# The second batch element's sums of weights begin only behind its token mixing

## The chip, the cores and the metric

One core of a Trainium2 chip. The metric is the device time of one execution, in microseconds (us); the median of the runs before is 1364.33. The core has a matrix engine (TensorE, PE), three engines for elementwise work (VectorE or DVE, ScalarE or ACT, GpSimd or POOL), a queue that only issues transfers (SyncE, SP), and sixteen DMA engines that carry the transfers out.

## What is computed

All numbers are float32. Twelve heads of attention with normalised queries and keys, for a batch of 8 elements of 448 positions, then a block that mixes over positions (tokens) and then over the 768 channels:

```python
# q, k, v: (8, 12, 448, 64)
q_n, k_n = rmsnorm(q, g_q), rmsnorm(k, g_k)
attn = softmax(q_n @ k_n.T / 8)
x = (attn @ v), heads side by side          # (8, 448, 768)
h = relu(x.T @ w_tok1) @ w_tok2             # token mixing, width 256
u = x + h.T
out = u + relu(u @ w_ch1) @ w_ch2           # channel mixing, width 1536
```

## The kernel before

The kernel works through the batch elements one after the other. While element b goes through token and channel mixing, the attention of element b + 1 is computed beside it. The order of the instructions on PE, DVE, ACT and POOL is written out by the program: work is cut into items, each a pair of a cost in us and a function that emits instructions. `merge` (L27) deals several lists of items into one so that each advances in proportion to its total cost. `run` (L120) emits a list, and emits outputs and bridge transfers that were put off with `later` when the sum of costs has passed their time. SP's instructions are put in order by the framework, by when their waits can be met. Each transfer, whether SP or ACT issues it, uses one of eight completion counters in turn, and waits until the previous transfer on that counter has landed.

From the second element on, channel mixing uses a scheme of seven half-size products in place of eight (`PRODUCTS`, L648). For it the four quarters of each weight matrix must also be combined into four sums and differences. The first element still multiplies by the plain quarters; meanwhile the weights are stored to device memory by quarters (slots 0 to 3). `sum_items` (L196) makes the combined slots (4 to 7) of 36 weight pieces, in 39 items. Item i loads piece i (L203, 256 KB, into one of five buffers of `raw_pool`), combines piece i - 2 with three POOL instructions (L206, L207, L209), and stores piece i - 3 (L211, 256 KB). Items 0 to 5 run at the end of the first element's main stage, items 6 to 11 with its last items, items 12 to 32 and then 33 to 38 beside the second element.

Weights in use are read back from device memory in units of 384 KB by `load_units` (L676, transfer L687), up to five units ahead of the one in use; a unit with combined weights isn't loaded ahead before its pieces are stored.

The stages of an element from the second on:

- token mixing: `tok1` (matmul L629, then a Relu on ACT, L632), in two halves, and six `tok2` (matmul L637, then an addition into the element's state by DVE, L642). After every second one, `moving_sums` (L650) makes combinations of the state, two on DVE and two on POOL (L660, L661). The turned output of the element before (DVE, L855) is stored by ACT in four transfers each (L577). This part is the list `begin`, but for the first half of `tok1`, which runs ahead of it.
- channel-up: 21 items `ch1` (L749, matmul L761), three groups of seven products, each with two or three combinations on DVE, POOL and ACT (L766 and others). This is the list `early`.
- channel-down: 14 items `ch2` (L803, matmul L818) for two thirds of the columns (the list `double`), and 7 for the last third.

Beside these run attention's steps: scores (L334), their exponentials on ACT (L338), values (L408), row sums of the exponentials on POOL and DVE (es, L376), and for later heads the loads of q, k and v (L1071, L287) and the inverse root mean squares: squares on ACT (L1090), a reduction (L1104), halves put together (L1112, L1121) and a Newton iteration (L1126 to L1147) on DVE. PE's results of both mixings go through two PSUM buffers (`ps_M`, L99).

Of the kernel before, what the change touches and what calls it, by code (L numbers as in the profile page):

```python
# [26 lines left out]
def merge(*lists):  # L27

    totals = [sum(c for c, _ in l) or 1.0 for l in lists]
    done = [0.0] * len(lists)  # L30
    at = [0] * len(lists)
    res = []
    while True:
        live = [i for i in range(len(lists)) if at[i] < len(lists[i])]
        if not live:
            return res
        i = min(live, key=lambda i: (done[i] + lists[i][at[i]][0] / 2) / totals[i])
        c, fn = lists[i][at[i]]
        at[i] += 1
        done[i] += c  # L40
        res.append((c, fn))
# [3 lines left out]
def whole(ctx, tc, shifted, pre, q, k, v, g_q, g_k, moe_w_tok1, moe_w_tok2, moe_w_ch1, moe_w_ch2, out):  # L45
# [74 lines left out]
    def run(items):  # L120
        for c, fn in items:
            fn()
            clock[0] += c
            while pending and pending[0][0] <= clock[0]:
                pending.pop(0)[1]()
# [70 lines left out]
    def sum_items():  # L196


        def one(i):
            n = len(stages)  # L200
            if i < n:
                t = st["sum", i] = raw_tile()
                nc.sync.dma_start(out=eight(t)[:, 0:4], in_=slots(i, 0, 4))  # L203
            if 0 <= i - 2 < n:
                q = eight(st["sum", i - 2])
                nc.gpsimd.tensor_tensor(out=q[:, 6], in0=q[:, 1], in1=q[:, 0], op=ALU.subtract)  # L206
                nc.gpsimd.tensor_tensor(  # L207
                    out=q[:, 4:6], in0=q[:, 1:7:5], in1=q[:, 3:4].to_broadcast([P, 2, P]), op=ALU.add)
                nc.gpsimd.tensor_tensor(out=q[:, 7], in0=q[:, 2], in1=q[:, 5], op=ALU.subtract)  # L209
            if 0 <= i - 3 < n:  # L210
                nc.sync.dma_start(out=slots(i - 3, 4, 8), in_=eight(st.pop(("sum", i - 3)))[:, 4:8])  # L211
                st["summed"] = i - 3 if i - 3 < n - 1 else n
                load_units(st["at"])

        def eight(t):
            return t[:].rearrange("p n w -> p (n w)").bitcast(F32).rearrange("p (q n) -> p q n", q=NQ)
        return [(1.0, lambda i=i: one(i)) for i in range(len(stages) + 3)]
# [43 lines left out]
    def weight_items(lo, hi):  # L261

        def one(i):
            if 3 <= i and i + 2 < len(chunks):
                weight_load(i + 2)
            convert_bits(i - 2)
            if i < len(chunks):
                convert_first(i)
            if 0 <= i - 1 < len(chunks):
                convert_second(i - 1)  # L270
            if 0 <= i - 2 < len(chunks):
                convert_last(i - 2)
            if 0 <= i - 3 - len(first):
                store(i - 3 - len(first))
        return [(1.0, lambda i=i: one(i)) for i in range(lo, hi)]
# [582 lines left out]
    def turns(b, cs):  # L858
        return [(0.3, lambda cc=cc: trans_y(b, cc)) for cc in cs]
# [3 lines left out]
    def x_items(b, h):  # L863
        return [(0.1, lambda j=j: trans_x(b, j)) for j in range(h * NC // 2, (h + 1) * NC // 2)]

    def tok1_items(b, h):
        return [(us(NS, HC), lambda j=j, h=h: tok1(b, j, h)) for j in range(NJ)]

    def middle_items(b):

        items = []
        for t in range(KC):
            items += [(us(NJ, S), lambda cc=cc: tok2(b, cc)) for cc in (t, KC + t)]
            if b:
                items.append((0.0, lambda t=t: moving_sums(b, t)))
        if b == 0:
            items += [(us(6, S), lambda mp=mp, o=o, j=j: ch1_first(mp, o, j))
                      for mp in range(KF // 2) for o in range(2) for j in range(2)]
            return items, [(us(6, S), lambda o=o, h=h, m=m: ch2_first(o, h, m))
                           for o in range(2) for h in range(2) for m in range(2)]  # L880
        items += [(us(6, HS), lambda mp=mp, i=i: ch1(b, mp, i)) for mp in range(KF // 2) for i in range(7)]
        return items, [(us(6, HS), lambda i=i, j=j: ch2(b, 0, i, j)) for i in range(7) for j in range(2)]

    def in_next(b):


        return b < B - 1 and not shifted

    def last_items(b, sums):

        single = [(us(6, HS), lambda i=i: ch2(b, 1, i, 0)) for i in range(7)]
        if b == 0:
            single = merge(
                [(us(6, S), lambda o=o, h=h: ch2_first(o, h, 2)) for o in range(2) for h in range(2)], sums)
        l = [] if in_next(b) else turns(b, [0, 1, KC, KC + 1])
        return [single[0]] + merge(single[1:-1], l) + [single[-1]]
# [52 lines left out]
    left, sums = [], sum_items()  # L949
    for b in range(B):  # L950
        early, double = middle_items(b)
        if b == 0:
            begin = x_items(0, 1) + tok1_items(0, 0) + tok1_items(0, 1)
            early = merge(begin + early, weight_items(BEFORE, then)) + merge(
                double, weight_items(then, len(chunks) + 3) + sums[:6])
        else:

            run(merge(tok1_items(b, 0), left[:2]))
            begin, early = merge(tok1_items(b, 1) + early[:3 * KC], left[2:]), early[3 * KC:]
            if b == 1:  # L960
                early, double = merge(begin + early, sums[12:33]), merge(double, sums[33:])
                begin = []
            early = begin + early + double
        lo = (b + AHEAD) * per + 1
        att = []
        if b + AHEAD < B:
            att = att_items(lo, lo + 10) + x_items(b + AHEAD, 0) + att_items(lo + 10, lo + per)
        tail = 4
        early, last = early[:-tail], early[-tail:]
        if b + 1 < B:  # L970
            last = merge(last, x_items(b + 1, 1))
        run(merge(att, early) + last + last_items(b, sums[6:12]))
        left = turns(b, range(NC) if in_next(b) else [2, KC + 2])
# [182 lines left out]
def kernel(  # L1156
# [30 lines left out]
    with tc.If(nc.values_load(small[0:1, 0:1], min_val=0, max_val=1,  # L1187
                              skip_runtime_bounds_check_because="a comparison's result") > 0) as arm:
        whole(tc, False, pre, *args)
    with arm.Else():  # L1190
        whole(tc, True, pre, *args)
# [30 lines left out]
```

## Time and profile before

| | us |
|---|---|
| runs: median of 4 (lowest, highest) | 1364.33 (1355.04, 1370.91) |
| the profiled execution | 1367.82 |
| its span, first to last instruction | 1366.0 |
| PE busy, share of the span | 1287.4, 94% |
| DVE, POOL, ACT busy | 749.8, 369.7, 366.2 |
| mean traffic of the DMA engines | 175 GB/s |

The costliest groups of instructions that bear on the change, with their busy time in the whole span:

| group | times | busy us, mean ns |
|---|---|---|
| PE, channel-down products (L818) | 1764 | 343.9, 355 |
| PE, channel-up products, moving side from the combinations (L761) | 1008 | 201.6, 355 |
| PE, `tok2` (L637) | 192 | 81.9, 567 |
| POOL, middle instruction of a sum (L207) | 36 | median 726 ns each |
| transfers: unit from device memory (L687) | 318 | 3.9 us from issue to landing |
| transfers: load of a piece (L203) | 36 | 4.7 us |
| transfers: store of a sum (L211) | 36 | 4.0 us |

How to read it: the times of a group are of one profiled execution. Idle time on an engine counts only where the chain of work that ends last goes through it, so a stage is judged by what PE waits for in it. The granted clock is the share of its full clock that PE had. The share of the DMA engines is the mean of the sixteen.

### The profile page before, as it was taken

What the parts mean: (1) busy time and instruction counts of PE and PEld (TensorE: products, weight loads), DVE (VectorE), ACT (ScalarE), POOL (GpSimd) and SP (SyncE); (2) the same over time, 40 slices, a digit from 0 to 9 for tenths busy, and PEclk for the clock granted to TensorE, in tenths of its full rate; (3) what the DMA queues carried; (4) which work ended last, traced back from release to release, by engine and by line L of the source; (5) the groups of instructions that cost most, each with busy time, mean ns of one, the idle gap of its engine ahead of it and who ended that gap; (6) DMA issues with size and microseconds to landing.
All of it is one profiled execution on the core that took longest, in us unless ns stands there. A gap on an engine that the chain in (4) does not pass through costs nothing.

```text
span 1366.0 us, 20203 instructions
## 1 busy us (share of the span) xinstructions
PE 1287.4 (94%) x7408; PEld 924.3 (68%) x7408; DVE 749.8 (55%) x1295; ACT 366.2 (27%) x734; POOL 369.7 (27%) x406
## 2 busy tenths in 40 slices
PE   4889999979998999999999999999999989999997
PEld 2344444437687578785888667785878758787997
DVE  6988987226773465626574275635566155443212
ACT  5553442023220243203331133302332023200100
POOL 1202110347662233203330132312341024211220
PEclk9999999999999999999999999999999999999998
DMA  9685878988899566694559755694667835375555
GB/s 202 187 242 169 243 184 214 248 209 212 240 245 229 125 163 149 152 231 89 145 132 212 173 131 140 154 225 97 161 168 162 213 71 162 111 185 149 180 165 122
DMA packets 508144, 238.83 MB, mean 175 GB/s; under 512 B 374084, under 2 KB 466628, under 8 KB 508036
## 3 DMA queue, kind: packets, MB, share of 16 engines
q1 hardware_dynamic: 416962, 225.97, 64.0%
q10 hardware_dynamic: 90946, 11.48, 5.3%
q8 instruction: 61, 1.00, 0.3%
q14 instruction: 47, 0.39, 0.1%
q0 software_dynamic: 128, 0.00, 0.0%
HBM read 197.85 MB, written 39.52 MB: 174 GB/s over the span
## 4 chain that ended last, share of the span: by engine, by line
PE 75%; DVE 8%; DMA 7%; SPq 2%; issue 2%; ACT 2%; ACTq 1%; POOL 1%; DVEq 0%; POOLq 0%
PE m_ps L761 23%; PE m_ps L818 19%; PE s_ps L334 8%; PE o_ps L408 7%; PE m_ps L629 6%; DMA unit<-ws 5%; PE m_ps L742 4%; PE m_ps L724 4%; PE m_ps L637 2%; SPq L1071 1%; PE d_ps L388 1%; ACTq L577 1%; DVE uT L642 1%; DMA ws<-raw 1%; DVE es L376 1%
## 5 line engine op out<-in xcount | busy, mean ns | idle before, releaser
L818 PE MATMUL m_ps<-hb,unit 128*128 128x224 f32 x1764 | 343.9, 355 | 18.1 <-DMA unit<-ws 17.6
L818 PEld LDWEIGHTS m_ps<-hb,unit 128*128 128x128 f32 x1764 | 330.7, 190 | 36.9 <-issue 30.1
L761 PE MATMUL m_ps<-tu,unit 128*128 128x224 f32 x1008 | 201.6, 355 | 2.7 <-DVE hb L766 2.4
L761 PEld LDWEIGHTS m_ps<-tu,unit 128*128 128x128 f32 x1008 | 188.9, 190 | 18.7 <-issue 5.6
L338 ACT ACTIVATE e<-s_ps 128x448 f32<-128x448 f32 x336 | 157.1, 547 | 133.8 <-PE s_ps L334 99.4
L761 PE MATMUL m_ps<-uT,unit 128*128 128x224 f32 x756 | 152.3, 355 | 0.3 <-DVE uT L642 0.3
L761 PEld LDWEIGHTS m_ps<-uT,unit 128*128 128x128 f32 x756 | 141.4, 190 | 14.8 <-DVE qkT L314 7.0
L334 PE MATMUL s_ps<-qkT 64*64 64x448 f32 x1260 | 148.2, 558 | 2.3 <-ACT x L609 1.7
L408 PE MATMUL o_ps<-e,v 64*64 64x448 f32 x1316 | 149.3, 540 | 0.1
L827 POOL TENSOR_TENSOR uT<-uT,r 128x448 f32<-128x448 f32 (+1 forms) x56 | 50.6, 914 | 278.0 <-DVE r L827 146.8
L827 DVE TENSOR_TENSOR uT<-uT,m_ps 128x448 f32<-128x448 f32 (+1 forms) x70 | 33.8, 500 | 144.9 <-PE m_ps L818 144.9
L766 DVE TENSOR_TENSOR r<-m_ps,r 128x448 f32<-128x448 f32 x63 | 39.2, 623 | 131.1 <-PE m_ps L761 80.8
L376 DVE TENSOR_TENSOR es<-es,e 128x896 f32<-128x896 f32 x84 | 97.3, 1159 | 10.3 <-ACT e L338 7.4
L637 PE MATMUL m_ps<-w_sb,h 128*128 128x448 f32 x192 | 81.9, 567 | 17.0 <-DVE uT L642 14.1
L408 PEld LDWEIGHTS o_ps<-e,v 64*64 64x64 f32 x1316 | 50.0, 133 | 68.2 <-issue 62.4
L376 POOL TENSOR_TENSOR es<-e 128x896 f32<-128x896 f32 x21 | 44.3, 2111 | 190.7 <-ACT e L338 190.7
L1104 DVE TENSOR_REDUCE ms<-sq 128x28 f32<-128x896 f32 (+2 forms) x47 | 51.3, 1091 | 81.0 <-ACT sq L1090 78.3
L334 PEld LDWEIGHTS s_ps<-qkT 64*64 64x64 f32 x1260 | 44.2, 135 | 74.3 <-issue 60.8
L629 PE MATMUL m_ps<-x,w_sb 112*128 112x384 f32 x256 | 86.0, 490 | 0.0
L766 POOL TENSOR_TENSOR hb<-r,r 128x448 f32<-128x448 f32 x21 | 23.8, 1135 | 225.4 <-ACT r L782 225.4
L637 PEld LDWEIGHTS m_ps<-w_sb,h 128*128 128x128 f32 x192 | 35.6, 194 | 60.1 <-DVE uT L642 28.9
L317 ACT ACTIVATE qkT<-qkT,g_t 128x448 f32<-128x448 f32 x36 | 24.0, 668 | 194.3 <-DVE qkT L314 182.9
(100 smaller groups left out, 1360.3 us busy)
## 6 DMA issues: line engine op xcount, KB each, us to landing
unit<-ws SPq DMA_DIRECT2D x318, 384.0 KB, 3.9
raw<-in_moe_w_ch_dram SPq DMA_DIRECT2D x72, 256.0 KB, 3.7
out_dram<-turned ACTq DMA_DIRECT2D x192, 56.0 KB, 1.9
v<-in_v_dram SPq DMA_DIRECT2D x94, 112.0 KB, 4.9
xs<-xt SPq DMA_DIRECT2D x56, 168.0 KB, 4.3
x<-xs SPq DMA_DIRECT2D x14, 672.0 KB, 7.3
ws<-stage SPq DMA_DIRECT2D x36, 256.0 KB, 3.9
raw<-ws SPq DMA_DIRECT2D x36, 256.0 KB, 4.7
```

The source lines that it names most:

```text
L334: nc.tensor.matmul(out=pss[i][rows_of(i, a), 0:S], lhsT=qkT[h, 1, k * D:(k + 1) * D], rhs=qkT[h, 0, :], start=True, stop=True)
L338: nc.scalar.activation(out=e[:, i, :], in_=pss[i][:, 0:S], func=AF.Exp)
L376: eng.tensor_tensor(out=es[:], in0=(es if k > 1 else st["e", t, 0])[:], in1=st["e", t, k][:], op=ALU.add)
L408: nc.tensor.matmul(out=st["o", p][a * D:(a + 1) * D, 0:S], lhsT=vt[rows, k * D:(k + 1) * D], rhs=e[rows, :], **kw)
L629: nc.tensor.matmul(out=ps[:, 0:HC], lhsT=w1_sb[0:R, c, jc * P:(jc + 1) * P], rhs=st["x", b, h][0:R, :, c, :], start=(c == 0), stop=(c == N ...
L637: nc.tensor.matmul(out=ps[:, 0:S], lhsT=st["h1", jc][:, cc * P:(cc + 1) * P], rhs=w2_sb[:, jc].rearrange("p c r -> p (c r)"), start=(jc == ...
L724: nc.tensor.matmul(out=ps[:, 0:S], lhsT=st["w"][t // KC][:, t % KC, j, :], rhs=u[:, t, :], start=(t == 0), stop=(t == 2 * KC - 1))
L742: nc.tensor.matmul(out=ps[:, 0:S], lhsT=w, rhs=natural(half)[:, :, t, :], start=(half == 0 and t == 0), stop=(half == 1 and t == KF - 1))
L761: nc.tensor.matmul(out=ps[:, j * HS:(j + 1) * HS], lhsT=w[:, t, j, :], rhs=m, start=(t == 0), stop=(t == KC - 1))
L766: add = lambda e, o, x, y: e.tensor_tensor(out=o, in0=x, in1=y, op=ALU.add)
L818: nc.tensor.matmul(out=ps[:, j * HS:(j + 1) * HS], lhsT=st["w"](j, t), rhs=hb[:, HB[what], t, :], start=(t == 0), stop=(t == KF - 1))
L827: add = lambda e, o, x, y: e.tensor_tensor(out=o, in0=x, in1=y, op=ALU.add)
```

## The change

The items 12 to 32 of the sums were dealt among the items of token mixing and channel-up together (`begin + early`); now they are dealt among those of channel-up alone, and token mixing stands ahead of them without any. Nothing is added or left out.

```diff
             run(merge(tok1_items(b, 0), left[:2]))
             begin, early = merge(tok1_items(b, 1) + early[:3 * KC], left[2:]), early[3 * KC:]
             if b == 1:
-                early, double = merge(begin + early, sums[12:33]), merge(double, sums[33:])
-                begin = []
+
+                early, double = merge(early, sums[12:33]), merge(double, sums[33:])
             early = begin + early + double
```

The joined list is then dealt together with the attention of the third element, `run(merge(att, early) + ...)` (L972), in which an item of the sums counts with a cost of 1.0.

## The prediction

> **What bounds the kernel now.** I read the page first: TensorE (PE) is busy 94% of the span, so only stages in which it is not can give or lose much. Then busy time by stage. The second batch element (b = 1) runs from 275.0 to 450.4 us; I cut it at its first token matmul (L629), first channel-up matmul (L761) and first channel-down matmul (L818), and its last stretch where no attention is left. The third element, which does the same work without sums, is cut alike. Columns: stretch, length, busy us of PE, its weight loads, VectorE (DVE), ScalarE (ACT), GpSimd (POOL), granted clock, busy share of the DMA engines, GB/s.
>
> ```profile
> 275.00:314.40 39.40, 32.30 (x146) 14.15 (x144) 17.07 (x34) 7.53 (x18) 18.51 (x24) 0.91 0.74 190
> 314.40:385.66 71.26, 67.92 (x433) 53.69 (x430) 44.60 (x67) 25.46 (x53) 47.08 (x63) 1.00 0.92 240
> 385.66:428.50 42.84, 42.31 (x264) 34.41 (x263) 30.94 (x46) 8.29 (x17) 21.96 (x25) 1.00 0.95 238
> 428.50:450.40 21.90, 16.67 (x84) 15.74 (x85) 2.71 (x7) 0.34 (x1) 2.58 (x4) 1.00 0.97 254
> ...
> 450.40:480.40 30.00, 29.05 (x145) 13.21 (x144) 16.41 (x34) 7.48 (x18) 8.45 (x6) 1.00 0.39 76
> 480.40:547.06 66.66, 66.66 (x433) 53.61 (x430) 39.92 (x68) 25.63 (x52) 22.66 (x16) 1.00 0.66 163
> ```
>
> Token mixing takes 39.4 us with sums beside it and 30.0 us without; channel-up 71.3 against 66.7. So the sums cost 9.4 us in the one and 4.6 in the other, and the DMA engines are almost full through the whole second element (0.92, 0.95, 0.97). Next the chain of waits through the hole in token mixing (start, us, what):
>
> ```profile
> 287.80 5.56 DMA unit<-ws
> 293.35 0.02 issue
> 293.37 3.71 DMA out_dram<-turned
> 297.08 0.94 ACT sq L1090
> ...
> 298.04 1.10 DVE ms L1104
> ...
> 302.54 0.54 DVE uT L642
> 303.08 0.04 issue
> 303.13 5.73 PE m_ps L637 x10
> ```
>
> PE stands still until 303.13 for the first addition of token mixing (L642). This is queued on DVE behind the reduction L1104 and a square-root chain, which wait for ACT's squares, which are queued behind ACT's issue of output stores; those wait for earlier transfers. Last, what SP, the queue of nearly all transfers, waits for in channel-up, second element, then third:
>
> ```profile
> SPq L687 <- PE m_ps L761: 5.0, 5, 1.9
> ...
> SPq L687 <- PE m_ps L761: 28.6, 13, 5.2
> ```
>
> A weight load that waits for PE to free its buffer is ahead of need: 28.6 us of that without sums, 5.0 with sixteen of them. The lead is nearly spent.
>
> **The change, part by part.** The built programs differ only between 285 and 386 us; each engine has the same instructions after as before.
>
> *Token mixing without sums.* Five POOL triples (L206, 207, 209: 0.45 + 0.73 + 0.45 us and gaps, 1.77 in all), four loads and five stores leave it. In both programs a transfer waits for the one eight places earlier among SP's and ACT's. ACT's third set of stores now waits, at its last, for the load of the first later sum, not for the second v load. That sum load takes the slot in which the first v load was issued at 291.11 (when a store had landed that stays where it is), and lands 4.6 us later by the median of its kind between 285 and 314: 295.7. With 0.4 to issue, the squares start at 296.1 and not 297.06, so L1104 ends at 298.1 and not 299.1. L642 now stands directly behind L1104 instead of behind the chain: its result is there at 298.7 and not 303.1. But the items are also dealt out anew: with no sums' cost in token mixing, one attention step goes from it into channel-up, and the step that filled PE from 294.4 to 298.9 stands two token matmul groups later. So PE waits from 294.4 to 298.7 with nothing. Then: third and fourth group 4.6 us at the 0.57 us per matmul of the chain's last row (second addition ready at about 301, in time for the fourth), attention 3.2, fifth and sixth group 3.4 at 0.42 us; channel-up starts at about 310.1, 4.3 before 314.4. It owes the attention step of 3.2 (311.23 to 314.40): gain 1.1 us. Bounds: 9.4 gained if token mixing becomes that of the third element, 3.2 lost if its hole stays as long as it is and the filler is gone.
>
> The clock belongs to that hole:
>
> ```profile
> 290.00:310.00 20.00, 13.45 (x49) 5.39 (x50) 10.48 (x23) 5.98 (x14) 12.24 (x14) 0.83 0.94 242
> ```
>
> Idle stretches of 2.9 and 4.2 us stand beside a granted clock of 0.83: 3.4 us lost out of 20. The hole that I foresee (4.3 us) is as long, so I keep 0.57 us per matmul and no gain. The Trainium skill, TensorE: Matmul & The Clock Gate, Part 1, puts the drop at one idle window of about 3.4 us, to half the clock; by it a hole cut below that would give back most of the 3.4 us, and the lost filler speaks against that.
>
> *Channel-up with more sums.* SP's loads and stores of sums planned in it go from 23 to 32: nine more of 256 KB, 2.36 MB. At 300 GB/s (the stretch from 290 to 300) they take 7.9 us of all DMA engines, at this stage's 240 GB/s 9.8; I take 8.8. The stage holds 0.92 x 71.3 = 65.6 us of DMA work, so 74.4. At the share of the next stage, 0.95, that is 78.3 us from 310.1, to 388.4 against 385.7 before: 2.7 later. At a share of 1.00 it is 384.5, a gain of 1.1, and PE's own 67.9 + 3.2 + its 3.3 idle gives the same; at 0.92 it is 391.0, 5.3 lost. SP's lead counts otherwise: nine issues at 71.3/91 = 0.78 us are 7.0, less 3.2 of longer stage, 3.8 out of a lead of 5.0, which just fits. I take 0.95: it is the nearest stage whose DMA is fuller, and what its queue does not finish is still owed where the share is 0.97.
>
> *POOL and who waits for it.* Five triples, 8.9 us, make 56 of 74 us there. Queued behind them are L766 (buffers r2 and hb), which DVE and through it PE's two PSUM buffers wait for, and es. The first L766 is due some 17 us into the stage, and the triples ahead of it are 8.9: nothing. Later seven triples, four sums of 1.13 and two es of 2.08 (21 us) stand against seven products and two attention steps of PE (23): nothing, up to 2.4 lost, the stage's largest wait for DVE (349.5), if that one comes a second time. It came where POOL and DVE were busy together:
>
> ```profile
> 300.92 0.22 DVE L1146 TENSOR_TENSOR nt<-nt,ms 128x56 f32<-128x56 f32 x1
> ...
> 344.13 0.77 DVE L1146 TENSOR_TENSOR nt<-nt,ms 128x56 f32<-128x56 f32 x1
> ```
>
> The same small multiplication takes 0.22 us with POOL idle and 0.77 beside triples. The Trainium skill, SBUF — State Buffer, Who interferes with whom, says that a DVE instruction with two SBUF inputs contends with a GpSimd instruction that reads SBUF, and the loser waits for the whole of it; by that alone an estimate is up to 8.9 us of DVE time moved to where it hurts. DVE is busy 44.6 of 71.3 us there, so I keep nothing to 2.4.
>
> *Weights in time.* The first weights that need the moved sums (second group) need the second of the five triples, done by about 315 and landed 4.2 later; their load is due at about 326. Nothing; without that cover, up to one landing of 4.9 us.
>
> The sum is 2.7 us. The profiled execution took 1367.82 (span 1366.0 and 1.8 around it), 3.5 above the median of 1364.33: 1370.5 on its base, 1367.0 on the median's.
>
> **The rivals.** *Faster:* token mixing becomes that of the third element, and channel-up swallows the sums in the prefetched weights. For it: 39.4 against 30.0. Against it: the hole is held by ACT's stores and weight loads, which mostly stay, and loses its filler. -9.4: 1355; with the 4.6 of channel-up too, -14.0: 1350.
>
> *Slower:* channel-up becomes bound by its transfers. It moves 17.1 MB at 240 GB/s; 19.46 MB at the same rate are 81.1 us, 9.9 more, and starts at 314.4 if token mixing is no shorter, with a second cold stretch of PE of 3.4 us as between 290 and 310: 13.3 later, 1378. It decides if 240 GB/s is already the ceiling of this mix of small packets; stretches of 300 GB/s and more within the stage speak against it, the lead of only 5.0 us for it.
>
> *Nothing:* 2.36 MB fit into the 5.7 us that the DMA engines have free in channel-up and the 3.2 it grows by: 1364.
>
> **How the numbers follow.** About 1% (13.6 us) is what a measurement of this kernel can tell; the four times of before spread over 15.9. Forecast 42%, slower rival 28%, faster rival 20%, nothing 10%. Of the faster rival's 20 I count 7 beyond 1%, the 13 others and both middle cases as no change, the slower rival as slower: faster 0.07, same 0.65, slower 0.28. The forecast's own range runs from -3 to +8 by the bounds above: 1361 to 1372. Reaching to the rivals, from 1355 to 1380, it leaves out about 2 in 10.
>
> **What would show it.** Right: L642's first result directly behind L1104; PE still idle about 4 us ahead of the third token group; channel-up starting some 4 us earlier and lasting some 78 us at a DMA share of 0.95 or more; SP's wait for PE in it near nothing. Wrong: no hole in token mixing (faster), or PE waiting for weights inside channel-up (slower), or a different time for anything after 450 us, where the programs are the same.

## The result, and the profile after

| | before | after |
|---|---|---|
| median of all runs, us (lowest, highest) | 1366.34 (1355.04, 1374.17) | 1369.75 (1362.68, 1377.07) |
| after over before | | 1.0027, interval 1.0015 to 1.0039 |
| profiled execution, its span, us | 1367.82, 1366.0 | 1365.74, 1364.0 |
| second element: token mixing, channel-up, channel-down, sum (that execution), us | 39.4, 71.3, 64.7, 175.4 | 36.5, 80.6, 62.4, 179.5 |

The ratio amounts to 3.7 us (2.0 to 5.3): slower, by less than 1%. The profiled execution of the changed kernel is 2.1 us shorter than that of the kernel before: a single execution can't show this change as a whole. It enters its second element 4.7 us earlier (270.3 against 275.0), after a stretch that both programs share. So I compare lengths of stages, and times counted from the start of the element. By these the second element is 4.1 us longer.

Busy time by stage of the changed kernel, cut and laid out as the table of before; the two last lines are the third element's token mixing and channel-up.

```profile
270.30:306.77 36.47, 28.13 (x113) 13.04 (x112) 12.70 (x29) 7.45 (x17) 10.12 (x12) 0.86 0.70 174
306.77:387.36 80.59, 74.83 (x462) 56.37 (x461) 48.75 (x72) 25.90 (x52) 63.72 (x79) 0.96 0.93 237
387.36:428.50 41.14, 41.14 (x261) 33.93 (x260) 28.13 (x45) 8.52 (x18) 18.72 (x21) 1.00 0.97 245
428.50:449.81 21.31, 17.69 (x90) 16.42 (x89) 2.87 (x7) 0.34 (x1) 2.58 (x4) 1.00 0.94 233
...
449.81:479.85 30.04, 29.09 (x145) 13.21 (x145) 16.45 (x34) 7.52 (x18) 8.45 (x6) 1.00 0.47 105
479.85:546.31 66.46, 66.46 (x432) 53.44 (x429) 39.73 (x68) 25.44 (x52) 22.47 (x16) 1.00 0.66 163
```

POOL's busy time in token mixing fell from 18.5 to 10.1 us, and yet the stage is nowhere near the 30.0 us of the third element: PE is busy for only 28.1 of 36.5 us, at a clock of 0.86 (0.91 before). Channel-up pays 9.3 us, and channel-down returns 2.3. The third element is as it was.

The chain of waits through the hole of token mixing (start, us, what):

```profile
286.86 5.68 DMA raw<-ws
292.54 0.02 issue
292.56 0.32 ACTq L577
...
292.99 0.96 ACT sq L1090
...
293.97 1.08 DVE ms L1104
295.05 0.54 DVE uT L642
295.59 0.04 issue
295.64 4.93 PE m_ps L637 x8
```

This is the order that the prediction gave: ACT's output store (L577) goes out when a load of a later sum has landed, then squares, the reduction, and L642 with nothing between. PE waited 5.5 us for it, and 2.8 us for a Relu (L632) shortly before. Then three slices of 10 us, in the columns of the first table:

```profile
290.00:300.00 10.00, 4.50 (x8) 2.20 (x8) 5.13 (x15) 1.89 (x5) 1.50 (x3) 0.55 0.72 172
300.00:310.00 10.00, 10.00 (x60) 5.99 (x59) 8.01 (x14) 2.38 (x5) 3.39 (x4) 1.00 0.30 48
310.00:320.00 10.00, 10.00 (x72) 7.08 (x74) 8.12 (x11) 2.87 (x6) 9.02 (x12) 1.00 0.43 118
```

The DMA engines stand at 0.30 and 0.43 just where the moved sums could have used them. SP's order of time, and what it waited for in channel-up (us in total, times, the longest), say why:

```profile
291.16 2.49 SPq L203 DMA_DIRECT2D raw<-ws  x2
309.24 0.33 SPq L687 DMA_DIRECT2D unit<-ws  x1
314.51 2.84 SPq L211 DMA_DIRECT2D ws<-raw  x2
```

```profile
SPq L687 <- PE m_ps L761: 13.2, 5, 11.2
SPq L211 <- POOL raw L209: 12.6, 7, 4.9
```

SP issues nothing from 293.7 to 309.2. For 11.2 us of this it stands at a weight load whose buffer PE has yet to free, and from 309.6 on at the store of a sum that POOL makes only now, because its item is now an item of channel-up (4.9 us to 314.5). SP issues in order, so everything else stands behind these two. From 320 us on the DMA engines are full. Whether this standstill is what makes channel-up long is another question; the experiments come back to it.

What PE waited for in channel-up, and the chain through the larger of the two:

```profile
PE o_ps L408 <- DMA v<-in_v_dram: 3.5, 1, 3.5
PE m_ps L761 <- DVE r L766: 2.2, 1, 2.2
```

```profile
372.98 5.78 DMA v<-in_v_dram
378.76 0.14 issue
378.89 2.23 PE o_ps L408 x4
```

A load of v comes late, for which PE did not wait before (its waits in channel-up were 2.4 us for L766, 0.6 and 0.3), and the granted clock is 0.88 from 370 to 380 and 0.78 from 380 to 390. The 9.3 us that channel-up is longer are 3.2 of the attention step, some 3.7 in which PE does the same work at a lower clock (busy 74.8 us against 67.9 + 3.2), and 2.4 more of waiting.

### The profile page after: what moved, and what is told of

Same layout as the page of the kernel before. It is cut to its first block, busy times and chain, and to the rows that moved or that the text cites. A ratio compares the mean times of both kernels' runs of the same rounds, so it can differ in the third digit from the quotient of the medians.

```text
span 1364.0 us, 20216 instructions
## 1 busy us (share of the span) xinstructions
PE 1287.2 (94%) x7408; PEld 924.8 (68%) x7408; DVE 746.6 (55%) x1295; ACT 366.4 (27%) x734; POOL 373.5 (27%) x406
## 4 chain that ended last, share of the span: by engine, by line
PE 72%; DVE 8%; DMA 8%; SPq 4%; issue 2%; ACT 2%; POOL 2%; ACTq 1%; DVEq 0%; POOLq 0%
PE m_ps L761 23%; PE m_ps L818 18%; PE o_ps L408 7%; PE s_ps L334 7%; PE m_ps L629 6%; DMA unit<-ws 4%; PE m_ps L742 4%; PE m_ps L724 4%; PE m_ps L637 2%; SPq L1071 2%; PE d_ps L388 1%; ACTq L577 1%; DMA ws<-raw 1%; DVE uT L642 1%; DVE raw L227 1%
## 5 line engine op out<-in xcount | busy, mean ns | idle before, releaser
L818 PE MATMUL m_ps<-hb,unit 128*128 128x224 f32 x1764 | 344.8, 355 | 13.4 <-DMA unit<-ws 13.2
L766 DVE TENSOR_TENSOR r<-m_ps,r 128x448 f32<-128x448 f32 x63 | 39.3, 623 | 138.7 <-PE m_ps L761 86.4
L1104 DVE TENSOR_REDUCE ms<-sq 128x28 f32<-128x896 f32 (+2 forms) x47 | 51.3, 1091 | 80.9 <-ACT sq L1090 78.3
L766 POOL TENSOR_TENSOR hb<-r,r 128x448 f32<-128x448 f32 x21 | 23.8, 1134 | 209.4 <-ACT r L782 209.4
L317 ACT ACTIVATE qkT<-qkT,g_t 128x448 f32<-128x448 f32 x36 | 24.0, 668 | 191.3 <-DVE qkT L314 179.8
```

Source lines behind the costliest of these rows:

```text
L766: add = lambda e, o, x, y: e.tensor_tensor(out=o, in0=x, in1=y, op=ALU.add)
L818: nc.tensor.matmul(out=ps[:, j * HS:(j + 1) * HS], lhsT=st["w"](j, t), rhs=hb[:, HB[what], t, :], start=(t == 0), stop=(t == KF - 1))
```

## The experiments

The table has the stage lengths of each profiled execution, in us, beside what the timed runs say against the kernel before. The columns mix, up and down are the second element's token mixing, channel-up, and channel-down whole; the cuts are at the first matmuls themselves, within 0.2 us of those above. A stage length is that of a single execution: two profiles of the changed kernel differ by up to 1.5 us in a stage, every other kernel has one, and that of e2 was the slowest of its twelve runs, 9.5 us above their median.

| run | mix | up | down | sum | ratio, interval | us |
|---|---|---|---|---|---|---|
| before | 39.5 | 71.1 | 64.9 | 175.6 | | |
| after | 36.5 | 80.5 | 62.5 | 179.5 | 1.0027 (1.0015, 1.0039) | +3.7 |
| e1 sums moved, attention not | 40.0 | 72.3 | 65.4 | 177.6 | 1.0004 (0.9986, 1.0022) | +0.5 |
| e2 attention moved, sums not | 36.7 | 73.0 | 69.6 | 179.4 | 1.0017 (1.0000, 1.0033) | +2.3 |
| e3 after, no POOL work | 35.8 | 79.4 | 62.3 | 177.5 | 1.0028 (1.0009, 1.0047) | +3.8 |
| e4 after, no sums' transfers | 36.2 | 74.2 | 65.4 | 175.8 | 0.9982 (0.9966, 0.9998) | -2.5 |
| e5 before, stores later | 29.0 | 87.6 | 65.2 | 181.9 | 1.0048 (1.0025, 1.0072) | +6.6 |
| e6 after, stores later | 25.6 | 99.2 | 64.3 | 189.2 | 1.0086 (1.0064, 1.0108) | +11.8 |
| e7 before, no attention in mixing | 21.8 | 112.3 | 63.3 | 197.4 | 1.0151 (1.0125, 1.0177) | +20.7 |
| e8 before, ten items in mixing | 37.7 | 75.2 | 62.9 | 175.8 | 1.0006 (0.9986, 1.0027) | +0.8 |
| e9 before, stores on SP | 31.6 | 70.2 | 64.2 | 165.9 | 0.9928 (0.9899, 0.9957) | -9.8 |
| e10 after, stores on SP | 26.4 | 81.7 | 61.4 | 169.5 | 0.9958 (0.9935, 0.9980) | -5.7 |
| e11 after once more | 37.9 | 81.7 | 61.6 | 181.3 | one run | |
| e12 after, one v load on ACT | 37.3 | 75.0 | 69.0 | 181.4 | 1.0012 (0.9990, 1.0034) | +1.6 |

**e1 and e2: the two parts of the change apart.** The change moves the sums, and with them, by the deal, one attention step. e1 moves the sums alone: their places in token mixing keep their cost, but emit nothing.

```diff
-                early, double = merge(early, sums[12:33]), merge(double, sums[33:])
+                mixed = merge(begin + early, sums[12:33])
...
+                head = [(c, (lambda: None) if f in fns else f) for c, f in mixed[:cut]]
+                early = head + merge(
+                    [it for it in mixed[cut:] if it[1] not in fns], [(n / 21, f) for _, f in sums[12:33]])
+                double, begin = merge(double, sums[33:]), []
```

> Sums as in the changed kernel (none in token mixing, 21 in channel-up), attention dealt as before. Theory A (the sums' transfers, taken out of token mixing, are owed in channel-up; the lost attention filler costs a little): token mixing 31 to 35 us with its filler back, channel-up 75 to 79 us, element as a whole +1 to +4 us on before. Theory C (the place of the attention step makes the loss): time as before, within 1 us. Theory B (GpSimd's triples in channel-up, beside VectorE, make the loss): as A in time, but channel-up long by waits for VectorE.

e2 moves the attention alone: the sums stay, at no cost in the deal as long as token mixing lasts.

```diff
-                early, double = merge(early, sums[12:33]), merge(double, sums[33:])
+                mixed = merge(begin + early, sums[12:33])
...
+                early = [(0.0 if f in fns else c, f) for c, f in mixed[:cut]]
+                early += [(21 / n if f in fns else c, f) for c, f in mixed[cut:]]
+                double, begin = merge(double, sums[33:]), []
```

> Sums where they were before, attention dealt as in the changed kernel. Theory A: the sums' place decides, so channel-up is 71.3 + 3.2 = 74 to 75 us, token mixing 36 to 40, time 0 to +2 us on before. Theory C: as the changed kernel, +3 to +5 us on before. Theory B: as before, within 1 us.

Measured: +0.5 us (-1.9 to +3.0) and +2.3 us (0 to 4.5), together 2.8, which lies within the 2.0 to 5.3 of the whole. Either may be the larger part; the intervals don't part them. One thing is plain: PE waits in token mixing for L642 and for the Relu in both (4.2 and 3.3 us; 5.2 and 2.9 us), so neither the sums nor the attention step makes the hole. And PE's wait for a late v load in channel-up, 3.5 us in the changed kernel, is 0.9 us in e2 and absent in e1: by these profiles it takes both moves.

**e3 and e4: POOL's work or the transfers.** e3 leaves out POOL's combining of the 21 pieces that go with items 12 to 32, and stores plain quarters in its place. e4 keeps POOL's work and leaves out 18 loads of pieces and 18 stores of sums (4.7 MB each way), and channel mixing reads plain quarters for the combined ones.

```diff
-            if 0 <= i - 2 < n:
+            if 0 <= i - 2 < n and not 10 <= i - 2 < 31:
...
```

> The changed kernel with the 21 sums in channel-up not computed: the loaded quarters are stored in their place (left out: the sums, so the products with them are of other weights). All transfers stay. Theory A: the transfers bind, so channel-up stays at 77 to 81 us and the time within 3 us of the changed kernel. Theory B: channel-up falls to 71 to 74 us, and the time to 3 to 7 us under the changed kernel.

```diff
+            if 12 <= i < 30:
+                st["sum", i] = st["kept"]
...
-                nc.sync.dma_start(out=slots(i - 3, 4, 8), in_=eight(st.pop(("sum", i - 3)))[:, 4:8])
+                t = st.pop(("sum", i - 3))
+                if not 12 <= i - 3 < 30:
+                    nc.sync.dma_start(out=slots(i - 3, 4, 8), in_=eight(t)[:, 4:8])
```

> The changed kernel with 18 of the sums computed on GpSimd from a tile that stays, without their loads and stores (left out: the real sums; units of combined weights are read from the plain quarters' places, as many bytes). Theory A: channel-up falls to 70 to 73 us (the third element's 66.7 and an attention step of 3.2), the rest of the element by 2 to 4 us, token mixing to 30 to 33 us; 10 to 18 us under the changed kernel. Theory B: channel-up stays at 77 to 81 us, less than 4 us under the changed kernel.

No price of POOL's work shows: 1.0028 (1.0009 to 1.0047) without it, 1.0027 with it; intervals as wide as these leave some 3 us open. The Trainium skill, SBUF — State Buffer, Who interferes with whom, has a VectorE instruction with two SBUF inputs contend with a GpSimd instruction that reads SBUF. What such a collision would look like is in the trace of before (0.77 us for 0.22), but no time of the whole is seen to hang on it here. All the transfers that e4 leaves out are worth 6 us (0.9982 against 1.0027): channel-up takes 74.2 us for 80.5, of which channel-down takes back 2.9 in the profiles. That is the price of 18 pieces' transfers in the changed kernel, not of the few that the change moves; the same edit was not run on the kernel before, so how much of the 6 us was paid there already isn't known. Token mixing stays at 36.2 us with waits of 4.7 and 3.0 us, though none of these transfers is left.

**e5 and e6: what makes the hole.** The one thing common to all of these is ACT, which issues the output stores of the first element there. e5 (on the kernel before) and e6 (on the changed one, by the same edit) deal the six turned outputs among the first two channel-up items of the second element.

```diff
-            run(merge(tok1_items(b, 0), left[:2]))
-            begin, early = merge(tok1_items(b, 1) + early[:3 * KC], left[2:]), early[3 * KC:]
+            put = [] if b == 1 and not shifted else left
+            run(merge(tok1_items(b, 0), put[:2]))
+            begin, early = merge(tok1_items(b, 1) + early[:3 * KC], put[2:]), early[3 * KC:]
+            if b == 1 and not shifted:
+                early = merge(early[:2], left) + early[2:]
```

> The kernel before, in which the six turned outputs of the first element (copies L855 and ACT's stores L577) no longer stand beside the second element's token mixing; they are dealt among its first two channel-up items. The sums stay as before. Theory S (the hole in token mixing is held by ACT, which waits to issue those stores while squares and Relus stand behind them): PE's wait ahead of the second addition (L642) falls from 4.2 us to under 1, token mixing takes 31 to 34 us instead of 39.4, and the whole is 4 to 7 us shorter, ratio 0.995 to 0.997. Theory P (the hole is held by the transfers of the sums and units themselves, whatever ACT issues): token mixing stays at 38 us or more, ratio 0.999 to 1.001. Theory T (the transfers are only put off, and the stage after pays for them as it does for the moved sums): token mixing 31 to 34 us, but channel-up 75 us or more instead of 71.2, ratio 0.999 to 1.002.

> The changed kernel (sums 12 to 32 only behind token mixing) with the same six outputs dealt among the first two channel-up items. Theory S: token mixing falls from 36.5 us to the 30.0 of the third element, within 1 us; channel-up keeps its 80.5 us or adds the stores, 80 to 83; against the kernel before the ratio is 0.997 to 1.000. Theory P: nothing of sums is left in token mixing but 6 to 11, so its hole stays if those hold it: 35 us or more, ratio 1.002 to 1.004, as the changed kernel. Theory T: token mixing 30 us, channel-up 85 us or more, ratio 1.002 to 1.005.

The hole goes with the stores, and no theory had them cost so much where they went. Stages of e5, and what ACT does as channel-up begins (start, us, what, and in brackets how long it had computed nothing and what ended that):

```profile
271.87:300.83 28.96, 28.94 (x145) 13.19 (x143) 13.27 (x26) 7.45 (x17) 18.89 (x25) 1.00 0.82 241
300.83:388.47 87.64, 73.50 (x432) 56.02 (x429) 48.51 (x75) 25.74 (x52) 48.04 (x64) 0.92 0.84 208
```

```profile
307.50 14.46 ACTq L577 DMA_DIRECT2D out_dram<-turned  x12
322.01 0.67 ACT L317 ACTIVATE qkT<-qkT,g_t 128x448 f32<-128x448 f32 x1 [14.06 <-DMA out_dram<-turned]
```

Token mixing is without a hole, PE busy for all of its 29.0 us at full clock, with the sums in it as before. In channel-up ACT spends 14.5 us on issuing twelve stores, the turned query (L317) stands behind them, and PE waits 9.8 us for it (18.9 us in e6). Theory S holds for the hole; for the time Theory T holds, at a price above its range.

**e7 and e8: other doses.** e7 (on before) gives the items of token mixing a cost of nothing, so that no attention stands between its products. e8 (on before) deals ten items of the sums into token mixing, and eleven into channel-up.

```diff
-                early, double = merge(begin + early, sums[12:33]), merge(double, sums[33:])
-                begin = []
+                mixed = merge(begin + early, sums[12:33])
+                cut = 1 + max(i for i, it in enumerate(mixed) if it[1] in [f for _, f in begin])
+                early = [(0.0, f) for _, f in mixed[:cut]] + mixed[cut:]
+                double, begin = merge(double, sums[33:]), []
```

> The kernel before with all its sums where they were, but the items of token mixing count as nothing when attention is dealt in, so that no attention step of PE stands between its products (the change moves one step out, this moves two or three). Theory A (the step that leaves is the filler of the hole, and what it takes from token mixing channel-up gets back at full length, so moving it can only lose): PE's waits in token mixing grow to 10 us or more together, token mixing takes 34 to 37 us, channel-up grows by 6 to 9 us to 77 to 80, ratio 1.001 to 1.004. Theory S' (attention's own steps on ACT and DVE are what makes the additions late, and without them the hole closes): token mixing 28 to 31 us, channel-up 77 to 80, ratio 0.997 to 1.000.

```diff
-                early, double = merge(begin + early, sums[12:33]), merge(double, sums[33:])
-                begin = []
+                early = merge(begin, sums[12:22]) + merge(early, sums[22:33])
+                double, begin = merge(double, sums[33:]), []
```

> The opposite dose of the change: the kernel before has five or so sums beside token mixing, the changed one none, this one ten (items 12 to 21), and eleven beside channel-up. Theory D (transfers that move out of a stage with idle transfer time into a fuller one cost the whole 6 us that the run without the sums' transfers showed, in proportion): channel-up 66 to 69 us instead of 71.2, token mixing 40 to 44, ratio 0.997 to 1.000. Theory E (before is near the best share, since token mixing is held by the same transfers): token mixing 45 us or more, ratio 1.002 to 1.006.

e7 loses nearly four times what was expected at the most. Token mixing ends before its own additions do, and PE then waits 12.4 us for L642 and 15.2 us for a copy (L770) on ACT. The chain of waits, cut to how one queue holds the other:

```profile
298.98 0.47 POOL raw L209
299.46 0.36 SPq L211
299.82 0.05 issue
299.87 0.60 SPq L287
300.52 4.09 DMA v<-in_v_dram
304.69 0.32 ACTq L577
305.05 3.84 DMA out_dram<-turned
308.90 0.65 DVE turned L855
309.55 0.52 DVE uT L642
```

A store on ACT waits for a v load of SP, which shares its completion counter; the v load stood on SP behind the store of a sum (L211), which POOL had to make first; the landed store frees the buffer that DVE's next turned output waits for, and L642 stands behind that. In this way ACT took 34 us for twenty stores. e8 shows no difference, clear of noise, for more sums in token mixing (+0.8, -1.9 to 3.7): D's 66 to 69 us in channel-up did not come, nor E's 45 in token mixing.

**e9 and e10: the stores on SP.** A change of the issuing queue, for the first element's outputs alone; the instructions on PE, DVE and POOL stay as they are, ACT only loses its issues, and SP's order is planned anew.

```diff
-            nc.scalar.dma_start(
+            (nc.scalar if b else nc.sync).dma_start(
```

> The kernel before, in which the turned outputs of the first element are stored by SP instead of ACT, at the same place of the program; nothing is moved on PE, DVE, ACT or POOL. Theory S (PE's hole is ACT standing in front of its squares, Relus and turned queries while it waits to issue these stores, and no engine computes behind SP): PE's waits in the second element's token mixing, 7.1 us before, fall under 1.5 us, the mixing takes 29 to 33 us instead of 39.4 at a clock of 1.00, channel-up keeps 71 to 75 us, ratio 0.994 to 0.998. Theory T (the stage is owed to its transfers, and 24 more issues on SP only move the wait to its weights or its v loads): token mixing is shorter too, but channel-up or channel-down take back as much, the three stages together 174 us or more, ratio 0.999 to 1.003.

> The changed kernel with the turned outputs of the first element stored by SP instead of ACT. Theory S: token mixing 25 to 28 us instead of 36.5 (it holds one attention step less than before) at a clock of 1.00, channel-up 78 to 82 us, the three stages 168 to 172 us, ratio against the kernel before 0.995 to 0.999. Theory T: channel-up 85 us or more, ratio 1.000 to 1.004. In both theories it is slower than the same edit on the kernel before, by 2 to 5 us, if the moved sums themselves cost what the run without their transfers showed; equal or faster, if the hole of token mixing was the only reason why sums moved out of it gained nothing.

Stages of e9, the first two of e10, and PE's waits in token mixing, before and in e9:

```profile
271.71:303.27 31.56, 29.19 (x146) 13.19 (x144) 17.77 (x34) 7.53 (x18) 19.80 (x26) 1.00 0.93 238
303.27:373.43 70.16, 69.01 (x433) 53.93 (x430) 42.38 (x67) 25.34 (x52) 49.02 (x63) 1.00 0.99 255
373.43:437.62 64.19, 59.25 (x349) 50.31 (x348) 33.84 (x52) 8.80 (x19) 23.95 (x29) 1.00 0.97 241
```

```profile
278.74:305.15 26.41, 25.86 (x113) 12.24 (x112) 12.70 (x29) 7.45 (x17) 10.17 (x12) 1.00 0.65 155
305.15:386.86 81.71, 74.72 (x461) 56.16 (x460) 48.40 (x72) 25.98 (x52) 63.88 (x79) 0.96 0.99 251
```

```profile
PE m_ps L637 <- DVE uT L642: 4.2, 1, 4.2
PE m_ps L637 <- ACT h L632: 2.9, 1, 2.9
...
PE m_ps L637 <- DVE uT L642: 2.3, 2, 1.3
```

e9 beats both kernels: 1353.65 us beside 1364.59, a ratio of 0.9928 (0.9899 to 0.9957), 9.8 us. The stages together are 9.7 us shorter than before, 7.9 of it in token mixing, where PE's waits fell from 7.1 to 2.3 us (under 1.5 was expected) and the clock is full. Together with e5 that shows the owner of the hole: ACT, which issues these stores. In e9 ACT waits for no transfer in token mixing; before it waited 6.8 and 4.8 us. With the hole gone, the change as a whole (sums and attention step) still costs: e10 is slower than e9 by 6.1 us in the medians, 4.1 by the two ratios and 3.6 in the stages, though the two intervals overlap a little. e10's token mixing is 5.2 us shorter, of which 3.2 is the attention step, and its channel-up 11.5 us longer. PE waits there for the same late v load (4.7 us) and for r (2.2 us) as in the changed kernel.

This bears on SP's standstill. The first line is SP's wait in e10's channel-up, where the changed kernel had 13.2 us, 11.2 in one piece; the other two are e1, in the same twenty us in which the DMA engines of the changed kernel stood at 0.30 and 0.43:

```profile
SPq L687 <- PE m_ps L761: 2.9, 7, 0.7
...
300.00:310.00 10.00, 6.82 (x13) 3.18 (x14) 9.00 (x22) 1.85 (x5) 1.72 (x3) 0.83 0.30 49
310.00:320.00 10.00, 10.00 (x65) 6.99 (x64) 9.37 (x15) 2.93 (x6) 5.86 (x6) 1.00 0.45 71
```

e10 is without the long wait and its channel-up takes 81.7 us; e1 has the idle DMA engines and its channel-up takes 72.3. In e3, too, SP waits for PE 3.2 us at the longest, the DMA engines are full from 300 to 330 us (1.04, 1.02, 1.08), and channel-up takes 79.4 us, with other waits of PE (2.5 us for L642, 2.4 for the copy L770). So the standstill is not shown to be what makes channel-up long.

**e11: the changed kernel once more.**

> The changed kernel once more, for a second profile. If the stage lengths of the first profile stand for it, token mixing is 36 to 37 us, channel-up 79 to 82, channel-down 61 to 64, and PE waits 2 to 3 us for ACT's Relu and 5 to 6 us for the addition L642; if one execution is no measure of a stage, one of them is off by 3 us or more.

Token mixing 37.9, channel-up 81.7, channel-down 61.6; waits of 3.0 and 4.8 us in token mixing, of 4.0 (v) and 2.2 us (r) in channel-up. Token mixing lies 0.9 outside what was expected and the wait for L642 0.2, no stage by 3 us: the readings stand, to 1.5 us.

**e12: the late v load.**

```diff
-            nc.sync.dma_start(
+            (nc.scalar if p == 17 else nc.sync).dma_start(
```

> The changed kernel with one pair of v loads of 28 (the one for which PE waits 3.5 and 4.0 us in the two profiles of the changed kernel) issued by ACT, where ACT comes to it some 6 us before SP does; SP issues it behind a weight load that waits for PE to free its buffer. Theory V (what channel-up pays beyond the attention step is this late load and the clock that PE loses in the hole): PE's wait for v falls under 0.5 us, channel-up takes 74 to 77 us instead of 80.5 and 81.7, at a clock of 0.98 or more instead of 0.96, ratio against the kernel before 0.998 to 1.0005. Theory T (the stage is as long as its transfers, the v load is only the first that shows it): channel-up stays at 79 us or more and PE waits for weights or later loads in its place, there or in channel-down, ratio 1.0015 to 1.004.

Channel-up and channel-down of e12, and PE's wait in the latter:

```profile
309.31:384.35 75.04, 72.55 (x462) 55.75 (x461) 48.38 (x71) 24.58 (x49) 57.82 (x74) 0.98 0.90 232
384.35:453.38 69.03, 60.80 (x349) 51.51 (x348) 31.59 (x53) 10.21 (x21) 25.47 (x31) 0.95 0.94 241
```

```profile
PE m_ps L818 <- DMA unit<-ws: 7.7, 3, 4.9
```

Each theory is right in one half. The wait for v is gone, and channel-up takes 75.0 us at a clock of 0.98, as V had it. But channel-down takes 69.0 us for 62, with one wait of 4.9 us for weights at its beginning, as T had it. The two stages together are 144.0 us, and 143.0 and 143.3 in the two profiles of the changed kernel. The ratio (0.9990 to 1.0034) fits both. By these profiles the late v load is the place where channel-up paid, and with the load on time channel-down pays instead; the timed runs are too close to show whether anything was saved.

## Why the prediction was right, and where its steps were not

The time (2.7 us more than before, against a measured 3.7; 1367.0 on a base of 1364.33, against 1369.75 beside 1366.34) and its sign came out of a sum whose terms were each off. The two terms of the sum were too small by 1.4 to 2.8 us and by 2.3 to 3.4, and a stage of which the prediction said nothing gave 2.3 to 3.3 back. That the sum came so close is luck.

*Token mixing.* The mechanism is as predicted: the order of L1104 and L642, the lost filler, the cold clock that stays, one attention step less. The size was not. Counted from the element's start, the load that ACT's stores wait for was issued at 16.6 us (predicted 16.1) and took 5.68 us (predicted 4.6), so the squares began at 22.7 and not at 21.1. PE's hole is 5.5 and 4.8 us and not 4.3, and the stage 36.5 and 37.9 us and not 35.1. Against 39.4 that is 2.9 or 1.5 us, less than the 3.2 of the attention step that left: the foreseen gain of 1.1 is a loss of 0.3 to 1.7. The step did name ACT's stores as what holds the hole. It did not ask what they would be worth on another queue.

*Channel-up.* The work of the DMA engines is right: 0.93 x 80.59 = 74.9 us, predicted 74.4, with eight more transfers of sums issued in the stage (38 for 30) and not nine. The length is not, 80.6 and 81.7 us against 78.3: the share is 0.93 and 0.90 and not 0.95. One sign failed outright, "SP's wait for PE in it near nothing", and with it "3.8 out of a lead of 5.0, which just fits". Without sums in token mixing SP ran ahead to a weight load without a buffer and stood there 11.2 us, in front of transfers that the DMA engines had room for: from 300 to 320 us they had 10 x 0.70 + 10 x 0.57 = 12.7 us free, more than the 8.8 that nine transfers take. But the stage is as long in e10 without this wait, so it isn't shown to be the price. What PE lost against the prediction's own sum for it (67.9 + 3.2 + 3.3 = 74.4 us) is 3.7 us at a lower clock and 2.4 of waiting; its forecast had put no clock loss and no late load into channel-up. The longest wait, 3.5 us, is for a v load; of v loads the prediction said nothing, only of weights, which were in time.

*POOL.* "Nothing to 2.4" holds at its lower end. PE waits for L766 once in each kernel, 2.4 us before and 2.2 after, and not a second time. The chain to the 2.2 us after doesn't come through POOL's queue in front of L766, as the prediction had it: it comes from a load of k, which SP issued behind the store of a sum that POOL had just made, and goes through the squares, the reduction L1104 and the Newton iteration on DVE, behind which L766 stands.

*Channel-down.* Nothing was predicted there. It returned 2.3 and 3.3 us, its waits for weights falling from 5.8 to 3.6 and 2.8. e12 shows the exchange from the other side: what channel-up doesn't wait for, channel-down does. e2 has a short channel-up and a long channel-down as well (73.0 and 69.6 us, with its sums where they were), so the moved sums alone don't explain it.

So the account of the change, by the stages of two executions: token mixing -3.0 and -1.6, channel-up +9.4 and +10.6, channel-down -2.4 and -3.3, together 3.9 and 5.7, and 2.0 to 5.3 by the timed runs. Of channel-up's part 3.2 is the attention step, which had hidden part of the hole and now hides nothing. The rest is PE's lower clock and its waits. Why they come is shown only so far: the wait for v takes both moves (e1, e2), and without 18 pieces' transfers it is gone and the clock is full (e4). How much of the 3.7 us belongs to the attention and how much to the transfers stays open: e1 and e2 are too close to each other.

*The rivals.* "Slower" described channel-up: it forecast 81.1 us at 240 GB/s and a second cold stretch of PE, and the stage took 80.6 at 237 GB/s with a clock down to 0.78. It failed on the rest, a token mixing no shorter and no relief afterwards, and that the transfers' rate bounds the stage isn't shown: they ran at 251 GB/s in e10 and 255 in e9. "Faster" named the right hole and the wrong owner: of its 9.4 us e9 fetches 7.9 in token mixing, with the sums left where they were. "Nothing" lies outside the interval.

## What to carry to other kernels

A hole in one stage needn't be made by what is densest there. Ask for which engine the chain waits, and what stands in its queue between the work that is due and the work it does: here 24 small output stores, held up by transfers of another queue. Moving these stores to another place moved the hole with them (e5, e6); issuing them from a queue that nobody computes behind took most of it away (e9). And don't take a free resource beside a standing queue for the cause: here the stage was as long in runs where that queue did not stand.

## What the runs showed of the hardware

- Issuing can cost an engine far more than the issue. Four stores in a row take ACT some 2 us when nothing holds them (2.1 and 2.4 in e6 and e5), but twelve took it 14.5 us in e5 and twenty 34 us in e7.
- Small holes cost the clock, or don't. The same wait of 2.2 us (for r, L766) in the two profiles of the changed kernel was followed by a granted clock of 1.00 in the one and of 0.75 to 0.82, for some 8 us, in the other; 2.40 us in e12 was followed by 0.77 to 0.81, and 2.39 us in the kernel before by 1.00. In e5 the ten us in which a wait of 9.8 us ended had 0.59. The Trainium skill, TensorE: Matmul & The Clock Gate, Part 1, has the clock halved after one idle window of about 3.4 us, with windows that run on regardless of the program. The scatter between equal holes fits windows of that kind; that a hole of 2.2 us is enough is not what the page says, and here the measurement decides.
- The third element's token mixing takes 30.0 us in both kernels with the same kind of stores on ACT, and PE's only wait in it is 1.0 us. With the DMA engines at 0.39 to 0.47 of their time four stores in a row take ACT 1.9 to 2.7 us. Of these two stages the cost of issuing shows only in the one with dense transfers.
